# Loading E alone on the hardware queues, F through the casting queue, one early layer matmul and a split last copy in a low-rank attention and hardswish kernel

## The chip, the cores and the metric

The kernel runs on one core of a Trainium2 chip. The metric is the device time of one execution in microseconds (us). The kernel before took 508.95 us (median of 3 runs, 508.8 to 509.43). Of each version one execution was also taken with the hardware profiler; its span, from the first to the last instruction, is about 2 us shorter than the time of that execution (506.4 us of 508.28 for the kernel before).

Engines are named as in the profile: PE is TensorE, PEld its weight loads, ACT ScalarE, DVE VectorE, POOL GpSimd and SP SyncE. "The software queue" is the DMA queue that GpSimd fills (q0); q1 and q10 are the hardware queues that SyncE and ScalarE issue to.

## The reference, cut to what matters

```python
# q, k, v: (8, 8, 1024, 64);  E, F: (64, 1024);  w_in: (512, 2048);  w_out: (2048, 512), all float32
k_proj = einsum('ks,bhsd->bhkd', E, k)
v_proj = einsum('ks,bhsd->bhkd', F, v)
attn   = softmax(q @ k_proj.T / 8)
x      = (attn @ v_proj), heads side by side: (8192, 512)
h      = x @ w_in
out    = (h * clip(h + 3, 0, 6) / 6) @ w_out
```

Nearly all the work is the two matmuls of the layer. Attention of a batch is computed while the layer of the batch before it runs. Only the first batch has nothing to hide behind: before its first layer matmul stand the loads of E, F, k, q, v and w_in, and a chain of small matmuls.

## The kernel before

E and F are loaded uncast into the two halves of one tile, one on each hardware queue. The copies cast both at once, and eight transposes turn both at once. Before that, 12 filler matmuls on a tile of ones keep TensorE working while the loads come.

```python
scratch = g_tile().rearrange("p f n -> p (f n)")
ef_f32 = scratch[:, :2 * S].bitcast(f32)
nc.sync.dma_start(out=ef_f32[:KP], in_=E)
nc.scalar.dma_start(out=ef_f32[KP:], in_=F)
# ... cut
def busy(n):
    ps = pmm()
    for _ in range(n):
        nc.tensor.matmul(ps, ones[:, :P], ones, start=True, stop=True)

busy(12)
# ... cut; the software queue casts float32 to bfloat16 as it loads:
for j in range(KO):
    load_pair("k", j)
    load_q0(0, slice(2 * j, 2 * j + 2))
    if j == 0:
        make_identity(nc, ident)
for j in range(KO):
    load_pair("v", j)
# ... cut: then w_in in seven slices, the rest of q, w_out in four, k, v, q of the next batch
nc.vector.tensor_copy(ef_raw[:, :S // 2], ef_f32[:, :S // 2])
nc.scalar.copy(ef_raw[:, S // 2:], ef_f32[:, S // 2:])
# ... cut: eight transposes into ef_ps, then
nc.vector.tensor_copy(e_t, ef_pv[:, 0])
for a in range(2):
    nc.scalar.copy(f_t[:, :, a, :], ef_pv[:, 1])
busy(2)
```

The first block takes the four pairs of heads in turn, with fillers where TensorE would stand:

```python
for j in range(KO):
    self.keys(j)
    if j > 1:
        sums(j - 2)
    self.queries(0, (j,))
    if j > 0:
        scores(j - 1)
    else:
        busy(1)
    self.keys_transposed(j)
    if j < 2:
        busy(1)
scores(KO - 1)
# ... cut: values, sums and products of the pairs
products(2)
self.vals(3, nc.scalar.copy)
busy(1)
products(3)
```

The last tile of rows is computed in two halves of 256 columns. VectorE copies the first out of PSUM, ScalarE the second, and each has a store of its own:

```python
for e, copy, dma in ((0, nc.vector.tensor_copy, nc.sync), (1, nc.scalar.copy, nc.scalar)):
    half = slice(e * d_model // 2, (e + 1) * d_model // 2)
    o_ps = pmm()[:, :d_model // 2]
    for fo in range(FO):
        nc.tensor.matmul(o_ps, g[:, fo, c * P:(c + 1) * P], w_out_sb[:, fo, half],
                         start=(fo == 0), stop=(fo == FO - 1))
    o_sb = opool.tile([P, d_model], f32, tag="o_sb", name="o_sb")[:, :d_model // 2]
    copy(o_sb, o_ps)
    dma.dma_start(out=o_dst[:, half], in_=o_sb)
```

The softmax here doesn't subtract the row's maximum and nothing guards it: scores larger than these inputs give would overflow.

Of the kernel before, what the change touches and what calls it, by code (L numbers as in the profile page):

```python
# [8 lines left out]
f32 = mybir.dt.float32  # L9
# [6 lines left out]
def kernel(  # L16
# [49 lines left out]
    def pmm():  # L66
        return ps_mm.tile([P, TOK], f32, tag="mm", name="mm")

    def pat():
        return ps_at.tile([P, TOK], f32, tag="at", name="at")  # L70
# [3 lines left out]
        return gpool.tile([P, FO, TOK], bf16, tag="g", name="g")  # L74

    scratch = g_tile().rearrange("p f n -> p (f n)")
    ef_f32 = scratch[:, :2 * S].bitcast(f32)
    nc.sync.dma_start(out=ef_f32[:KP], in_=E)
    nc.scalar.dma_start(out=ef_f32[KP:], in_=F)
    nc.scalar.preload_act_table_set("natural_log_exp_and_others")  # L80
    ones = consts.tile([P, TOK], bf16, name="ones")
    nc.vector.memset(ones, 1.0)
# [7 lines left out]
    def busy(n):  # L90
        ps = pmm()
        for _ in range(n):
            nc.tensor.matmul(ps, ones[:, :P], ones, start=True, stop=True)  # L93

    busy(12)

    def raw_tile(name):
        return kqv_pool.tile([P, H, SO, D], bf16, tag=name, name=name)
# [13 lines left out]
    for j in range(KO):  # L112
        load_pair("k", j)
        load_q0(0, slice(2 * j, 2 * j + 2))
        if j == 0:
            make_identity(nc, ident)
    for j in range(KO):
        load_pair("v", j)

# [9 lines left out]
        nc.gpsimd.dma_start(out=w_in_sb[:, :, lo:lo + n], in_=w_in_v[:, :, lo:lo + n])  # L129

    for lo, n in ((0, 128), (128, 128), (256, 256), (512, 256), (768, 256),
                  (1024, 512), (1536, 512)):
        load_w_in(lo, n)
    load_q0(1, slice(0, H))
    for i in range(SB):
# [4 lines left out]

    e_t = consts.tile([P, SO, KP], bf16, name="e_t")
    f_t = consts.tile([P, SO, 2, KP], bf16, name="f_t")
    ef_raw = scratch[:, 2 * S:3 * S]
    nc.vector.tensor_copy(ef_raw[:, :S // 2], ef_f32[:, :S // 2])
    nc.scalar.copy(ef_raw[:, S // 2:], ef_f32[:, S // 2:])
    ef_si = ef_raw.rearrange("r (si so) -> r so si", so=SO)
    ef_ps = pat().bitcast(bf16)
    for so in range(SO):
        nc.tensor.transpose(ef_ps[:, so * P:(so + 1) * P], ef_si[:, so, :], ident)
    ef_pv = ef_ps.rearrange("p (so e r) -> p e so r", so=SO, e=2)  # L150
    nc.vector.tensor_copy(e_t, ef_pv[:, 0])
    for a in range(2):
        nc.scalar.copy(f_t[:, :, a, :], ef_pv[:, 1])
    ef_t = [e_t, f_t[:, :, 0, :]]
    busy(2)

# [198 lines left out]
    class First:  # L355
# [67 lines left out]
            return self.quads(lambda r, h: self.vp[r:r + KP, h, :], t, j, alloc)  # L423


        def first_block(self):
            recs = {}

            def scores(j):
# [15 lines left out]
# [7 lines that stand above are left out]
                else:  # L452
                    busy(1)
                self.keys_transposed(j)
                if j < 2:
                    busy(1)
            scores(KO - 1)
            self.vals(0, nc.vector.tensor_copy)
# [6 lines left out]
            busy(1)  # L465
            products(2)
            self.vals(3, nc.scalar.copy)
            busy(1)
            products(3)


# [40 lines left out]
    def second_group(b, t, g, c, copy=None):  # L512
        o_dst = out_rows(b, t, c)
        if (b, t, c) == (B - 1, NB - 1, SB - 1):

            for e, copy, dma in ((0, nc.vector.tensor_copy, nc.sync), (1, nc.scalar.copy, nc.scalar)):
                half = slice(e * d_model // 2, (e + 1) * d_model // 2)
                o_ps = pmm()[:, :d_model // 2]
                for fo in range(FO):
                    nc.tensor.matmul(o_ps, g[:, fo, c * P:(c + 1) * P], w_out_sb[:, fo, half],  # L520
                                     start=(fo == 0), stop=(fo == FO - 1))
                o_sb = opool.tile([P, d_model], f32, tag="o_sb", name="o_sb")[:, :d_model // 2]
                copy(o_sb, o_ps)
                dma.dma_start(out=o_dst[:, half], in_=o_sb)
            return
        o_ps = pmm()
        for fo in range(FO):
            nc.tensor.matmul(o_ps, g[:, fo, c * P:(c + 1) * P], w_out_sb[:, fo, :],  # L528
                             start=(fo == 0), stop=(fo == FO - 1))
            if fo % SB == SB - 1:  # L530
                yield
        o_sb = opool.tile([P, d_model], f32, tag="o_sb", name="o_sb")
        (copy or nc.scalar.copy)(o_sb, o_ps)  # L533
        nc.sync.dma_start(out=o_dst, in_=o_sb)
# [8 lines left out]

    xT = x_tile()
    first = First(xT)
    first.first_block()
    x_next = x_tile()
    g = [g_tile(), g_tile()]


    def two_groups(xT, t, g, kos):
        tiles = [pmm(), pmm()]
        for part in kos:
            for fo in range(2):
                h_part(tiles[fo], xT, t, fo, part)
        for fo in range(2):
            h_out(tiles[fo], g, fo)

    two_groups(xT, 0, g[0], ((0, 1, 2), (3,)))
    for fo in range(2, FO):  # L560
        first_group(xT, 0, g[0], fo)
        if fo >= FO - 2:
# [10 lines left out]
    for i in range(SB + 1):  # L573
# [3 lines left out]
            first.second_scores()  # L577
        elif i < 3:
            first.second_values(2 * i - 2)
    two_groups(xT, 1, g[1], ((0, 1), (2, 3)))  # L580
    for fo in range(2, FO):
        first_group(xT, 1, g[1], fo)
        pop()
# [19 lines left out]
    for b in range(1, B):  # L603
# [33 lines left out]
        for t in range(NB):  # L637
# [3 lines left out]
            for fo in range(FO):  # L641
                if b < 3 and t == 0 and fo < 2:

                    if fo == 0:
                        two_groups(xT, t, g, ((0, 1, 2), (3,)))
                else:
                    first_group(xT, t, g, fo)
                pop()
# [47 lines left out]
```

## Time and profile before

| | before |
|---|---|
| time, median | 508.95 us |
| span of the profiled run | 506.4 us |
| PE busy | 499.8 us (99%) |
| first keys start | 8.08 us |
| layer matmuls start and go on without a stop | 20.70 us |
| last matmul ends to the end of the span | about 3.3 us |

A line of the timeline gives start and length in us, the engine, the source line, the operation, output and input tiles, the number of instructions, and in brackets how long the engine stood idle before and what released it.

All that TensorE waited for in the whole span, from the view of waits (waiter, what released it, us in total, times, longest):

```profile
PE mm L93 <- DVE halves L84: 1.5, 1, 1.5
PE mm L414 <- ACT aT L434: 0.6, 1, 0.6
PE mm L407 <- DVE kT L377: 0.3, 1, 0.3
PE mm L528 <- DVE g L501: 0.2, 1, 0.2
```

### The profile page before, as it was taken

Reading aid. Unit: us, or ns where it says so; the run is one execution under the profiler, and the core shown is the slowest. Engines: PE = TensorE matmul, PEld = TensorE weight load, DVE = VectorE, ACT = ScalarE, POOL = GpSimd, SP = SyncE. Lnnn points to the kernel's source line nnn. Section 1 sums busy time; section 2 is a strip of 40 time slices with the busy share of each in tenths; the row PEclk is TensorE's granted clock in tenths of the full one; section 3 lists DMA queues with packets and bytes.
Section 4 is the critical chain, followed back from the end, with each engine's and each line's share of the span. In section 5 each row is a group of like instructions: output and inputs, shape, how many; then the busy total and the mean of one; then the engine's idle time right before and its main releaser. Section 6 shows DMA issues by size and latency. Waiting matters only on the chain.

```text
span 506.4 us, 7084 instructions
## 1 busy us (share of the span) xinstructions
PE 499.8 (99%) x2779; PEld 225.3 (44%) x2779; DVE 246.2 (49%) x384; ACT 256.2 (51%) x438; POOL 37.9 (7%) x57
## 2 busy tenths in 40 slices
PE   8999999999999999999999999999999999999997
PEld 4444444444444444444444444444444444444444
DVE  3572836865733564536635455534652446334420
ACT  3656466567565444654555544654455544434431
POOL 8610020020020020010002000000000000000000
PEclk9999999999999999999999999999999999999999
DMA  9999999599299998699316990248110361101112
GB/s 168 200 205 207 204 153 238 104 151 190 86 154 187 271 150 168 137 160 256 107 43 130 215 263 30 60 99 208 41 43 29 84 159 43 41 22 42 43 42 83
DMA packets 77529, 66.02 MB, mean 130 GB/s; under 512 B 36200, under 2 KB 66664, under 8 KB 77496
## 3 DMA queue, kind: packets, MB, share of 16 engines
q0 software_dynamic: 31952, 29.36, 37.1%
q1 hardware_dynamic: 45320, 35.82, 27.1%
q10 hardware_dynamic: 224, 0.39, 0.3%
q8 instruction: 21, 0.34, 0.3%
q14 instruction: 12, 0.10, 0.1%
HBM read 69.73 MB, written 16.94 MB: 171 GB/s over the span
## 4 chain that ended last, share of the span: by engine, by line
PE 96%; ACT 2%; DVE 1%; issue 0%; ACTq 0%
PE mm L528 43%; PE mm L495 43%; PE at L195 2%; PE mm L93 1%; PE at L244 1%; PE at L226 1%; PE mm L244 1%; PE mm L520 1%; PE mm L264 1%; ACT aT L235 0%; PE at L382 0%; PE at L414 0%; PE mm L226 0%; PE at L394 0%; PE mm L195 0%; PE at L366 0%
## 5 line engine op out<-in xcount | busy, mean ns | idle before, releaser
L501 DVE SCALAR_TENSOR_TENSOR g<-r,mm 128x512 bf16<-128x512 f32 x256 | 174.5, 687 | 176.3 <-ACT r L500 175.6
L495 PE MATMUL mm<-xT,w_in_sb 128*128 128x512 bf16 x1024 | 231.0, 379 | 0.3
L528 PE MATMUL mm<-w_out_sb,g 128*128 128x512 bf16 x1008 | 230.4, 379 | 0.2 <-DVE g L501 0.2
L500 ACT ACTIVATE r<-mm 128x512 f32<-128x512 f32 x256 | 152.3, 599 | 76.9 <-PE mm L495 75.7
L495 PEld LDWEIGHTS <-w_in_sb 128*128 128x128 bf16 x1024 | 99.3, 98 | 122.6 <-issue 4.0
L528 PEld LDWEIGHTS <-g 128*128 128x128 bf16 x1008 | 96.8, 98 | 120.3 <-issue 7.0
L533 ACT COPY o_sb<-mm 128x512 f32<-128x512 f32 x55 | 32.1, 586 | 124.0 <-PE mm L528 124.0
L257 DVE TENSOR_TENSOR xT<-at,rec 128x512 bf16<-128x512 f32 x42 | 26.5, 682 | 6.5 <-ACT rec L176 6.5
L235 ACT ACTIVATE aT<-at 128x512 bf16<-128x512 f32 x38 | 20.2, 615 | 9.1 <-PE at L226 9.1
L201 DVE CAST kp<-at 64x512 bf16<-64x512 f32 x12 | 7.7, 677 | 15.5 <-PE at L195 15.5
L216 POOL COPY mark<-qT 1x1 bf16<-1x1 bf16 x4 | 0.7, 177 | 161.6 <-DMA qT<-q 161.6
L235 ACT ACTIVATE aT<-mm 128x512 bf16<-128x512 f32 x18 | 10.3, 613 | 3.6 <-PE mm L226 3.6
L533 DVE COPY o_sb<-mm 128x512 f32<-128x512 f32 x8 | 5.5, 687 | 13.4 <-PE mm L528 13.4
L195 PE MATMUL at<-v,f_t 128*64 128x512 bf16 x48 | 11.5, 382 | 0.0
L195 PE MATMUL at<-k,e_t 128*64 128x512 bf16 x48 | 11.5, 382 | 0.0
L257 DVE TENSOR_TENSOR xT<-mm,rec 128x512 bf16<-128x512 f32 x14 | 9.0, 685 | 4.3 <-PE mm L244 4.3
L176 ACT ACTIVATE rec<-rec 128x1024 f32<-128x1024 f32 x10 | 10.6, 1061 | 0.3
L170 ACT ACTIVATE rec<-mm 128x512 f32<-128x512 f32 x10 | 5.5, 595 | 7.9 <-PE mm L244 5.4
L93 PE MATMUL mm<-ones 128*128 128x512 bf16 x19 | 7.8, 539 | 1.5 <-DVE halves L84 1.5
L170 ACT ACTIVATE few<-mm 128x512 f32<-128x512 f32 x10 | 5.4, 594 | 7.4 <-PE mm L264 7.4
L195 PEld LDWEIGHTS <-e_t 128*64 128x64 bf16 x56 | 5.6, 109 | 6.6 <-issue 1.9
L204 DVE CAST vp<-at 64x512 bf16<-64x512 f32 x12 | 8.3, 694 | 0.4
(75 smaller groups left out, 161.9 us busy)
## 6 DMA issues: line engine op xcount, KB each, us to landing
out_dram<-o_sb SPq DMA_DIRECT2D x63, 256.0 KB, 2.7
rec<-rows SPq DMA_DIRECT2D x40, 256.0 KB, 6.3
k<-in_k_dram POOLq DMA_DIRECT2D x7, 1024.0 KB, 14.2
v<-in_v_dram POOLq DMA_DIRECT2D x7, 1024.0 KB, 21.1
q<-in_q_dram POOLq DMA_DIRECT2D x7, 1024.0 KB, 10.3
w_out_sb<-in_moe_w_out_dram POOLq DMA_DIRECT2D x4, 512.0 KB, 17.3
k<-in_k_dram POOLq DMA_DIRECT2D x4, 256.0 KB, 5.4
v<-in_v_dram POOLq DMA_DIRECT2D x4, 256.0 KB, 7.7
```

Of the source, the lines that this page charges most:

```text
L93: nc.tensor.matmul(ps, ones[:, :P], ones, start=True, stop=True)
L170: nc.scalar.activation(rec[:, i], den, AF.Ln)
L176: nc.scalar.activation(flat, flat, AF.Exp, scale=-1.0)
L195: nc.tensor.matmul(ps[e * KP:(e + 1) * KP], ef_t[e][:, so, :], kqv[self.b]["kv"[e]][:, :, so, :], start=(so == 0), stop=(so == SO - 1))
L235: nc.scalar.activation(self.aT[j][:, r].rearrange("p a n -> p (a n)"), tiles[r], AF.Exp, scale=scale)
L244: nc.tensor.matmul(tiles[t][c:c + D].rearrange("p (r n) -> p r n", r=2), stationary(r, 2 * j + a), self.aT[j][r:r + KP, :, a, :], start=Tr ...
L257: nc.vector.tensor_mul(self.xT[:, j, t, :], av[t], rec[:, t])
L495: nc.tensor.matmul(h_ps, w_in_sb[:, ko, fo * P:(fo + 1) * P], xT[:, ko, t, :], start=(ko == 0), stop=(ko == KO - 1))
L500: nc.scalar.activation(r, h_ps, AF.Relu, bias=0.5, scale=1.0 / 6.0)
L501: nc.vector.scalar_tensor_tensor(g[:, fo, :], r, 1.0, h_ps, op0=ALU.min, op1=ALU.mult)
L528: nc.tensor.matmul(o_ps, g[:, fo, c * P:(c + 1) * P], w_out_sb[:, fo, :], start=(fo == 0), stop=(fo == FO - 1))
L533: (copy or nc.scalar.copy)(o_sb, o_ps)
```

## The change

The intent is to shorten the two ends. At the head, E alone uses both hardware queues, so that its transposes start sooner; F, which is needed only for values, goes through the casting software queue behind the first pair. Three of the 12 fillers go and two come in later. One layer matmul takes the place of the filler before the last values. At the tail, two engines share the last copy.

```diff
-    ef_f32 = scratch[:, :2 * S].bitcast(f32)
-    nc.sync.dma_start(out=ef_f32[:KP], in_=E)
-    nc.scalar.dma_start(out=ef_f32[KP:], in_=F)
+    for half, dma in zip(e_half, (nc.sync, nc.scalar)):
+        dma.dma_start(out=e_f32[:, half], in_=E[:, half])
...
-    busy(12)
+    busy(9)
...
             make_identity(nc, ident)
+            nc.gpsimd.dma_start(out=f_raw, in_=F)
...
-                  (1024, 512), (1536, 512)):
+                  (1024, 256), (1280, 256), (1536, 512)):
...     (E cast by both engines and transposed alone)
+    nc.vector.tensor_copy(e_t, with_sequence_on_partitions(e_raw))
+    busy(2)
+    def f_transposed():
+        ps = with_sequence_on_partitions(f_raw)
+        for a in range(2):
+            nc.scalar.copy(f_t[:, :, a, :], ps)
     busy(2)
...     (in the first block)
-                if j < 2:
+                if j == 0:
+                    f_transposed()
+                elif j < 2:
                     busy(1)
...
-            busy(1)
+            meanwhile()          # early[0].part(0, (0,)): one layer matmul
             products(3)
...     (the last tile)
-            for e, copy, dma in ((0, nc.vector.tensor_copy, nc.sync), (1, nc.scalar.copy, nc.scalar)):
+            ways = (nc.vector.tensor_copy, nc.sync), (nc.scalar.copy, nc.scalar)
+            for lo, pieces in ((0, ((0, half),)), (half, ((0, quarter), (quarter, half)))):
...
+                for (start, end), (copy, dma) in zip(pieces, ways):
+                    copy(o_sb, o_ps[:, start:end])
```

More of the change, by code (lines that the diff above doesn't have):

```diff
@@ L76 @@
     scratch = g_tile().rearrange("p f n -> p (f n)")
-    ef_f32 = scratch[:, :2 * S].bitcast(f32)
-    nc.sync.dma_start(out=ef_f32[:KP], in_=E)
-    nc.scalar.dma_start(out=ef_f32[KP:], in_=F)
+    e_f32 = scratch[:KP, :2 * S].bitcast(f32)
+    e_raw, f_raw = scratch[:KP, 2 * S:3 * S], scratch[:KP, 3 * S:4 * S]
+    e_half = [slice(i * S // 2, (i + 1) * S // 2) for i in range(2)]
+    for half, dma in zip(e_half, (nc.sync, nc.scalar)):
+        dma.dma_start(out=e_f32[:, half], in_=E[:, half])
     nc.scalar.preload_act_table_set("natural_log_exp_and_others")
@@ L142, with with_sequence_on_partitions @@
     f_t = consts.tile([P, SO, 2, KP], bf16, name="f_t")
-    ef_raw = scratch[:, 2 * S:3 * S]
-    nc.vector.tensor_copy(ef_raw[:, :S // 2], ef_f32[:, :S // 2])
-    nc.scalar.copy(ef_raw[:, S // 2:], ef_f32[:, S // 2:])
-    ef_si = ef_raw.rearrange("r (si so) -> r so si", so=SO)
-    ef_ps = pat().bitcast(bf16)
-    for so in range(SO):
-        nc.tensor.transpose(ef_ps[:, so * P:(so + 1) * P], ef_si[:, so, :], ident)
-    ef_pv = ef_ps.rearrange("p (so e r) -> p e so r", so=SO, e=2)
-    nc.vector.tensor_copy(e_t, ef_pv[:, 0])
-    for a in range(2):
-        nc.scalar.copy(f_t[:, :, a, :], ef_pv[:, 1])
+    for half, copy in zip(e_half, (nc.vector.tensor_copy, nc.scalar.copy)):
+        copy(e_raw[:, half], e_f32[:, half])
+    def with_sequence_on_partitions(raw):
+        ps = pat().bitcast(bf16)[:, :SO * KP]
+        for so in range(SO):
+            nc.tensor.transpose(ps[:, so * KP:(so + 1) * KP], raw.rearrange("r (si so) -> r so si", so=SO)[:, so, :],
+                                ident[:KP, :KP])
+        return ps.rearrange("p (so r) -> p so r", so=SO)
+    nc.vector.tensor_copy(e_t, with_sequence_on_partitions(e_raw))
[4 more added lines that the diff above has]
+            nc.scalar.copy(f_t[:, :, a, :], ps)
     ef_t = [e_t, f_t[:, :, 0, :]]
@@ L423, in values, with first_block @@
             return self.quads(lambda r, h: self.vp[r:r + KP, h, :], t, j, alloc)
-        def first_block(self):
+        def first_block(self, meanwhile):
             recs = {}
@@ L514, in second_group @@
         if (b, t, c) == (B - 1, NB - 1, SB - 1):
-            for e, copy, dma in ((0, nc.vector.tensor_copy, nc.sync), (1, nc.scalar.copy, nc.scalar)):
-                half = slice(e * d_model // 2, (e + 1) * d_model // 2)
-                o_ps = pmm()[:, :d_model // 2]
+            half, quarter = d_model // 2, d_model // 4
+            ways = (nc.vector.tensor_copy, nc.sync), (nc.scalar.copy, nc.scalar)
+            for lo, pieces in ((0, ((0, half),)), (half, ((0, quarter), (quarter, half)))):
+                o_ps = pmm()[:, :half]
                 for fo in range(FO):
-                    nc.tensor.matmul(o_ps, g[:, fo, c * P:(c + 1) * P], w_out_sb[:, fo, half],
+                    nc.tensor.matmul(o_ps, g[:, fo, c * P:(c + 1) * P], w_out_sb[:, fo, lo:lo + half],
                                      start=(fo == 0), stop=(fo == FO - 1))
-                o_sb = opool.tile([P, d_model], f32, tag="o_sb", name="o_sb")[:, :d_model // 2]
-                copy(o_sb, o_ps)
-                dma.dma_start(out=o_dst[:, half], in_=o_sb)
+                for (start, end), (copy, dma) in zip(pieces, ways):
+                    o_sb = opool.tile([P, d_model], f32, tag="o_sb", name="o_sb")[:, :end - start]
+                    copy(o_sb, o_ps[:, start:end])
+                    dma.dma_start(out=o_dst[:, lo + start:lo + end], in_=o_sb)
             return
@@ L545, with __init__, part, parts @@
     first = First(xT)
-    first.first_block()
-    x_next = x_tile()
-    g = [g_tile(), g_tile()]
-    def two_groups(xT, t, g, kos):
-        tiles = [pmm(), pmm()]
-        for part in kos:
-            for fo in range(2):
-                h_part(tiles[fo], xT, t, fo, part)
-        for fo in range(2):
-            h_out(tiles[fo], g, fo)
-    two_groups(xT, 0, g[0], ((0, 1, 2), (3,)))
+    g = [g_tile(), g_tile()]
+    class TwoGroups:
+        def __init__(self, xT, t, g):
+            self.xT, self.t, self.g = xT, t, g
+            self.tiles = [pmm(), pmm()]
+        def part(self, fo, kos):
+            h_part(self.tiles[fo], self.xT, self.t, fo, kos)
+        def parts(self, *kos):
+            for some in kos:
+                for fo in range(2):
+                    self.part(fo, some)
+            self.out()
+        def out(self):
+            for fo in range(2):
+                h_out(self.tiles[fo], self.g, fo)
+    early = []
+    def meanwhile():
+        early.append(TwoGroups(xT, 0, g[0]))
+        early[0].part(0, (0,))
+    first.first_block(meanwhile)
+    x_next = x_tile()
+    early[0].part(0, (1, 2))
+    early[0].part(1, (0, 1, 2))
+    for fo in range(2):
+        early[0].part(fo, (3,))
+    early[0].out()
     for fo in range(2, FO):
@@ L579 @@
             first.second_values(2 * i - 2)
-    two_groups(xT, 1, g[1], ((0, 1), (2, 3)))
+    TwoGroups(xT, 1, g[1]).parts((0, 1), (2, 3))
     for fo in range(2, FO):
@@ L644 @@
                     if fo == 0:
-                        two_groups(xT, t, g, ((0, 1, 2), (3,)))
+                        TwoGroups(xT, t, g).parts((0, 1, 2), (3,))
                 else:
```

## The prediction

> **What bounds the kernel now.** I read the page's busy shares first, then the chain that ended last, then TensorE's waits, and only then the two ends of the span.
>
> ```profile
> PE 499.8 (99%) x2779; PEld 225.3 (44%) x2779; DVE 246.2 (49%) x384; ACT 256.2 (51%) x438; POOL 37.9 (7%) x57
> PE 96%; ACT 2%; DVE 1%; issue 0%; ACTq 0%
> ```
>
> TensorE (PE) is busy 99% of 506.4 us, and 96% of the chain runs through it. TensorE's waits over the whole span add up to 2.6 us, of which 1.5 us is the wait before its first instruction. So nothing in the middle, from about 21 to 500 us, can give much, and the diff changes nothing there. Only the head and the tail are left. The head in the chain, in order of time (start us, us, what):
>
> ```profile
> 1.46 5.30 PE mm L93 x12
> 6.76 0.81 PE at L149 x8
> ...
> 7.60 0.44 DVE e_t L151
> ...
> 8.08 0.63 PE at L366 x8
> ...
> 19.45 0.57 PE at L382 x8
> ...
> 20.05 0.28 ACT vp L385
> ...
> 20.36 0.40 PE at L414 x2
> 20.77 7.45 PE mm L495 x34
> ```
>
> L93 are filler matmuls that only keep TensorE working; they are "busy" without being work, which is why 99% hides a head. The real chain is: E and F land, are cast, are transposed (L149), copied (e_t), keys (L366) and so on, until the layer's matmuls (L495) start and never stop. What the change is worth is how much sooner L495 runs without a stop. What feeds the head is seen in the loads (time to landing last) and in the queues of the stretches 2.0 to 3.4, 3.4 to 4.4 and 4.4 to 5.0 us (packets, MB, share):
>
> ```profile
> g<-in_F_dram ACTq DMA_DIRECT2D x1, 256.0 KB, 5.0
> w_in_sb<-in_moe_w_in_dram POOLq DMA_DIRECT2D x1, 128.0 KB, 9.5
> ...
> q1 hardware_dynamic: 57, 0.23, 90.2%
> ...
> q10 hardware_dynamic: 58, 0.24, 97.9%
> ...
> q0 software_dynamic: 83, 0.08, 84.5%
> ```
>
> E (q1) moves first, then F (q10), and only behind them the software queue with k, q, v and the weights. F was issued at 0.74 us, so it landed at 5.74. The software queue then runs full until past 30 us, at some 205 GB/s of what it writes. The first slice of w_in was issued at 10.67 us and landed near 20.2; it is used at 20.70. So **the head has a second bound close beside TensorE: the software queue**. Issue plus landing time against first use gives small slack everywhere: third key pair 10.4 against 11.46, fourth 12.4 against 13.08, third value pair 17.0 against 17.84, fourth 18.15 against 19.39, first w_in slice 20.2 against 20.70, the slice for groups 8 to 11 27.0 against about 27.6.
>
> **What the Trainium skill says.** "TensorE: Matmul & The Clock Gate", Part 1, says that TensorE starts at half its clock and is released after a free-running window of some 3.4 us in which it was busy. The trace agrees: fillers start every 0.43 us up to 6.13 us, and two after 7.39 us are 0.22 us apart; the release came near 7.37 us. Part 4 of that page says that transposes do not count as busy in the same way; this trace does not test it. "DMA: Bandwidth & Descriptors", section "Issuing engines are not separate DMA queues", says that DMAs from different engines run on the same 16 DMA engines. The trace agrees: E and F, issued together, moved one after the other. The same page, "SWDGE vs HWDGE vs iDMA", says that only GpSimd's DMA can cast, which is why F's cast load goes behind the first key pair there.
>
> **The change part by part.**
>
> 1. E alone, in halves on both hardware queues. E's packets were done near 3.75 us and F's near 4.86; F's landing was seen at 5.74, 0.9 us later. With E alone the last packet is near 3.7 us, so I estimate landing at 4.6. The casts (VectorE 0.66 us, ScalarE 0.62; same length along the row, half the partitions) end at 5.26. Nine fillers end at 1.46 + 9 x 0.427 = 5.30, which fits. The eight transposes start near 5.30 in place of 6.57: **1.27 us earlier**.
>
> 2. Part of that is given back at once. The clock is still at half there. Eight transposes at 0.107 us bring TensorE to 6.16; then stand four fillers in place of two: three at half clock, the last partly at full, until about 7.62. Keys follow there instead of at 8.08: **0.46 us earlier**. (e_t, ready at about 6.8, is not the limit then.) Had the clock been released earlier, fillers would be 0.22 us each and it would be up to 1.0; later, about 0.3.
>
> 3. F's own eight transposes replace one filler after the first keys: about 8 x 0.056 = 0.45 us (key matmuls' spacing at full clock) against 0.22 us and 0.1 us of idling there: 0.13 us lost. The two f_t copies (1.07 us on ScalarE) move from 8.06 to about 9.7 and end near when the first exponential needs ScalarE (11.01 before). **Net so far 0.33 us.** From there to the values the order is the same, so it is carried on.
>
> 4. The software queue. It starts after E instead of after F: some 0.8 to 1.1 us sooner. It then carries F itself, 256 KB read, 0.62 us at the rate of E's packets (4 x 0.155 us per DMA engine). Starting sooner it may also run thin at first, so I take a net shift of 0.3 us earlier for all behind F. w_in's first slice then lands near 19.9. GpSimd's issue for F (0.74 us) delays later issues, but they were 2 us or more ahead of their turn.
>
> 5. One layer matmul (0.216 us) replaces the filler before the last values, under the wait for the copy of vp (0.28 us). It is real work done where a filler ran: **0.22 us gained**, if w_in's first slice has landed. The copy would be done near 20.0; the slice lands at 19.9, so the matmul ends near 20.12 and costs about 0.1 us. Rest of L495 then near 20.46 with one already done: 0.24 + 0.22 = **about 0.45 us of head**.
>
> 6. Splitting the 512-column slice of w_in lets groups 8 and 9 start on 256 columns: removes a wait that would arise (slack 0.6 us before) and is worth nothing by itself.
>
> 7. The tail:
>
> ```profile
> 501.43 0.42 DVE L523 COPY o_sb<-mm 128x256 f32<-128x256 f32 x1 [14.30 <-PE mm L520]
> ...
> 503.16 0.37 ACT L523 COPY o_sb<-mm 128x256 f32<-128x256 f32 x1 [2.91 <-PE mm L520]
> 503.56 0.35 ACTq L524 DMA_DIRECT2D out_dram<-o_sb  x1
> ```
>
> The last copy (0.37 us for 256 columns on ScalarE) becomes 128 columns on each of two engines. From 512 columns 0.586 and 256 columns 0.37, 128 columns is about 0.26 on ScalarE; on VectorE (0.687, 0.42) about 0.29. Gain **0.08 us**; the bytes to store are the same, in packets of half the size, so the store (1.8 us to landing) gains nothing sure. I take 0.1.
>
> Sum: 0.45 + 0.1 = 0.55, and with some chance that the queue or clock is kinder, 0.65 us. 508.95 - 0.65 = **508.3 us**.
>
> **The rivals.**
>
> A. *Full gain.* The 1.27 us of the head reach the end, with 0.22 and 0.1 added: 1.6 us, 507.35. For it: three fillers gone and no other long wait. Against it: two more fillers, F's transposes back in the chain, and w_in's first slice, which no part of the change brings 1.3 us sooner. I give this or near it 8%.
>
> B. *The software queue takes the place of the wait removed.* F now stands in it ahead of three key pairs. If the queue does not start sooner, because GpSimd's descriptors are not ready, everything behind F lands 0.6 us later: w_in's first slice near 20.8. The early layer matmul would then hold up the last values behind it, and the head would be 0.3 to 0.4 us longer: 509.2. For it: slack of 0.5 to 1 us only. Against it: other starts of this queue in the trace show packets 1.6 us after the issue, so at 1.24 + 1.6 = 2.8 us it was ready and had to wait behind F. 12%.
>
> C. *The clock.* Fewer matmuls lie in the window that released the clock (9 fillers, transposes, then 4). If that window no longer counts as busy, the release comes 3.4 us later, near 10.8, and the work between costs about 1.2 us more: 509.6. The two added fillers speak against it. 10%.
>
> D. *All hidden.* Were the software queue the only bound, only parts 4, 5 and 7 count: 0.3 + 0.1, 508.5. That is inside my range.
>
> **Range and chances.** 2% is 10.2 us, and the whole head and tail that the change touches are some 20 us and 3 us, almost all of it work that stays. No rival comes near 2%: within 2% has 0.99. The three runs before spread over 0.6 us, which the moving clock window may cause. The range 507.6 to 508.95 holds the middle case, D and part of A, and leaves B and C outside on the slow side.
>
> **What would show it.** Transposes of E should start near 5.3 us and the first keys near 7.6; F should land before 8.5 us; the first w_in slice near 19.9, with TensorE at most 0.3 us idle before the early layer matmul; L495 unbroken from about 20.5. In the middle each matmul group takes as long as before. The last copies should take 0.26 and 0.29 us. The prediction is wrong if E lands after 5 us, if the fillers at full clock start only after 10 us, or if slices of w_in hold up L495.

## More of the kernel before

The timeline of the kernel before, TensorE alone, at four places that the change is to move: first keys, third keys, first layer matmuls, and the first projection of the second batch's values.

```profile
8.08 0.63 PE L366 MATMUL at<-k,e_t 128*64 128x128 bf16 x8
...
11.46 0.63 PE L366 MATMUL at<-k,e_t 128*64 128x128 bf16 x8
...
20.70 1.04 PE L495 MATMUL mm<-xT,w_in_sb 128*128 128x512 bf16 x4
...
55.29 0.40 PE L195 MATMUL at<-v,f_t 128*64 128x512 bf16 x1
```

None of the four has a bracket: TensorE went from one to the next without waiting there.

## The result

The changed kernel took **509.67 us** (median of 6 runs, 508.91 to 511.92), against 508.88 us for the kernel before in 6 runs (507.95 to 509.43). The ratio is **1.0026**, with a 95% interval of 1.0002 to 1.0049. Ratios here are the mean time of one kernel's fast runs over that of the other's of the same rounds, so they are not quite the ratio of the medians. By the 2% rule this is "same", as expected. But the time is above the range: the change costs about 0.8 us by the medians where 0.65 us was to be gained.

The six runs are of two kinds. Four had a mean granted clock of 1.0 and took 508.91 to 509.84 us; two had 0.99 and took 511.12 and 511.92 us. All count as fast runs of one core. Averaged, the four are 0.57 us above the mean of before (509.34 against 508.77); the two slow ones bring the mean to 1.30 us above it. So there are two losses to explain. (The first turns out to have two parts, one in the loads and one in the tail, after the end of the span.)

The profile after is of a run at full clock (509.1 us, span 507.0). TensorE at the same four places, with one more wait (9.94) and with the keys beside the second batch's values (55.28), in its timeline:

```profile
7.25 0.63 PE L376 MATMUL at<-k,e_t 128*64 128x128 bf16 x8
...
9.94 0.40 PE L404 MATMUL at<-ident,q 128*128 128x128 bf16 x4 [0.19 <-DMA q<-in_q_dram]
...
11.45 0.61 PE L376 MATMUL at<-k,e_t 128*64 128x128 bf16 x8 [0.72 <-DMA k<-in_k_dram]
...
20.83 3.41 PE L507 MATMUL mm<-xT,w_in_sb 128*128 128x512 bf16 x15
...
55.28 0.40 PE L205 MATMUL at<-k,e_t 128*64 128x512 bf16 x1
55.94 0.38 PE L205 MATMUL at<-v,f_t 128*64 128x512 bf16 x1 [0.26 <-DMA v<-in_v_dram]
```

The first keys start 0.83 us sooner. By the third keys that is gone: 11.45 against 11.46 us, after a wait of 0.72 us for a load. The layer runs on from 20.83 us with one matmul done before it (20.70 before, with none). That is not yet a loss: at the first transposes in the middle of the layer (33.58 us, 33.66 before) this execution is 0.08 us ahead. It loses at 55.94 us, where the profile before has no wait. The bracket there, 0.26, counts only from the modelled end of the matmul before; the first matmul of the values starts 0.66 us after that of the keys, where before both start at 55.29. The layer goes on at 57.76 us (57.14 before), and that is the whole 0.6 us by which this span is the longer one. Other executions lose at other loads: in the profiles of e1, e4 and e8 nothing waits near 55 us, but the same transposes start at 34.81, 34.80 and 34.21 us.

TensorE's waits for loads in the changed kernel, from the view of waits:

```profile
PE at L376 <- DMA k<-in_k_dram: 0.7, 1, 0.7
...
PE at L205 <- DMA v<-in_v_dram: 0.3, 1, 0.3
...
PE at L404 <- DMA q<-in_q_dram: 0.2, 1, 0.2
```

The third pair of keys, as issued and with its time to landing, in the kernel before and then after (timeline of GpSimd, and the loads):

```profile
4.72 0.73 POOL L110 DMA_DIRECT2D k<-in_k_dram  x1
...
k<-in_k_dram POOLq DMA_DIRECT2D x1, 256.0 KB, 5.7
```

```profile
5.29 0.72 POOL L112 DMA_DIRECT2D k<-in_k_dram  x1
...
k<-in_k_dram POOLq DMA_DIRECT2D x1, 256.0 KB, 6.0
```

It landed at 4.72 + 5.7 = 10.4 us before, and at 5.29 + 6.0 = 11.3 us after: 0.9 us *later*, although the queue's first packet moved at 3.05 us in place of 4.45.

In the trace the semaphore of each load goes up 16 times; I read this as once for each of the 16 DMA engines when its share has landed. TensorE goes on only after the last (third keys: 11.32 us, start at 11.45). These increments (us; first engine / eighth / last):

| load | before | after |
|---|---|---|
| first keys | 6.13 / 6.22 / 6.46 | 4.80 / 4.88 / 5.55 |
| second keys | 8.10 / 8.29 / 8.38 | 7.48 / 7.71 / 8.73 |
| third keys | 10.04 / 10.21 / 10.38 | 9.99 / 10.41 / 11.32 |
| fourth values | 17.83 / 18.00 / 18.19 | 17.92 / 18.29 / 19.41 |
| first w_in slice | 18.56 / 18.73 / 20.14 | 18.66 / 19.02 / 20.13 |
| second batch's values | 51.37 / 51.58 / 53.76 | 51.76 / 52.52 / 55.90 |

The head start of 1.3 us at the first keys is lost by the third even for the first engine. F's load, estimated at 0.62 us in the prediction, would explain half of that. The other half, and the spread between the engines, comes with single packets that take long. Of the software queue's packets before 20 us, 17 took over 0.4 us after the change (up to 1.37 us, most of them around 6 and 8 us), and none before it.

The tail, in the changed kernel's timeline:

```profile
503.79 0.29 DVE L537 COPY o_sb<-mm 128x128 f32<-128x128 f32 x1 [1.32 <-PE mm L533]
...
504.16 0.27 ACT L537 COPY o_sb<-mm 128x128 f32<-128x128 f32 x1 [3.29 <-DVE o_sb L537]
504.46 0.35 ACTq L538 DMA_DIRECT2D out_dram<-o_sb  x1
```

The two copies do not run side by side: ScalarE's waits for VectorE's, since both read one PSUM tile (with a tile each, in e3 below, it waits for TensorE alone). The last store is issued 0.76 us after the last matmul (503.70), not 0.48 us as before. It is half as large, and the span ends sooner after its issue (2.54 us in place of 2.81), so within the span the whole tail is about 3.3 us long in both. What follows the span is another matter (e1 and e2).

### The profile page after: what moved, and what is told of

It is laid out like the page before. It is cut to its first block, busy times and chain, and to the rows that moved or that the text cites. A ratio compares the mean times of both kernels' runs of the same rounds, so it can differ in the third digit from the quotient of the medians.

```text
span 507.0 us, 7049 instructions
## 1 busy us (share of the span) xinstructions
PE 495.7 (98%) x2733; PEld 225.5 (44%) x2784; DVE 246.3 (49%) x385; ACT 256.1 (51%) x438; POOL 39.2 (8%) x59
## 4 chain that ended last, share of the span: by engine, by line
PE 86%; DMA 9%; POOL 2%; issue 1%; ACT 1%; DVE 1%; DVEq 0%; ACTq 0%; POOLq 0%
PE mm L542 41%; PE mm L507 38%; DMA v<-in_v_dram 7%; PE at L205 2%; DMA w_in_sb<-in_moe_w_in_dram 2%; PE at L254 1%; PE at L236 1%; PE mm L254 1%; PE mm L533 1%; POOL q L108 1%; PE mm L274 1%; POOL k L112 1%; ACT aT L245 0%; PE mm L236 0%; PE mm L205 0%
## 5 line engine op out<-in xcount | busy, mean ns | idle before, releaser
L542 PE MATMUL mm<-w_out_sb,g 128*128 128x512 bf16 x985 | 227.6, 379 | 1.9 <-issue 1.0
```

## The experiments

Medians are of 5 or 6 runs, each beside runs of the kernel before on the same chip in the same rounds.

| run | median, us | before there, us | ratio to before (95%) |
|---|---|---|---|
| changed kernel, first measurement | 509.67 | 508.88 | 1.0026 (1.0002 to 1.0049) |
| e8, changed kernel again | 509.05 | 508.53 | 1.0010 (0.9998 to 1.0023) |
| e1, changed, old tail | 508.85 | 508.02 | 1.0006 (0.9992 to 1.0020) |
| e2, before, new tail | 508.88 | 508.02 | 1.0007 (0.9992 to 1.0022) |
| e4, changed, 12 fillers | 509.18 | 508.02 | 1.0011 (0.9997 to 1.0024) |
| e5, changed, F behind the keys | 510.31 | 508.02 | 1.0039 (1.0024 to 1.0055) |
| e7, changed, F on a hardware queue | 508.68 | 508.53 | 0.9994 (0.9979 to 1.0010) |
| e9, before, early layer matmul | 508.62 | 508.53 | 0.9998 (0.9985 to 1.0011) |
| e11, changed, more fillers | 508.91 | 508.53 | 1.0005 (0.9992 to 1.0017) |
| e3, before, tail in two tiles | 508.63 | 508.13 | 1.0003 (0.9989 to 1.0017) |
| e10, e9 and that tail | 508.36 | 508.13 | 0.9999 (0.9986 to 1.0013) |
| e12, changed, F loaded twice | 509.18 | 508.13 | 1.0030 (1.0009 to 1.0051) |
| e13, e7 and that tail | 508.14 | 508.13 | 0.9999 (0.9983 to 1.0016) |
| e14, before, half loads (wrong result) | 508.11 | 508.47 | 0.9995 (0.9976 to 1.0014) |
| e15, changed, half loads (wrong result) | 507.13 | 508.47 | 0.9971 (0.9955 to 0.9987) |

### The tail: e1 and e2

In e1 the changed kernel gets back the tail of before; in e2 the kernel before gets the new tail.

```diff
 e1: the changed kernel
-            for lo, pieces in ((0, ((0, half),)), (half, ((0, quarter), (quarter, half)))):
+            for e, copy, dma in ((0, nc.vector.tensor_copy, nc.sync), (1, nc.scalar.copy, nc.scalar)):
 e2: the kernel before, the other way round
```

> The changed kernel with the tail of before. In the changed kernel's profile the two last copies ran one after the other (0.29 us, then 0.27 us), but the smaller last stores landed sooner, so the tail as a whole came out about even. Theory (the tail is not the loss): within 0.15 us of the changed kernel, so 0.3 to 1 us slower than before. Rival (the tail is the loss): as fast as before or 0.3 us faster than it. In both, the first keys still start near 7.3 us and the third keys wait for their load.

> The kernel before with the new tail alone. Theory (tail about even): within 0.2 us of before. Rival (the serial copies cost): 0.3 us or more slower than before. The profile should show ScalarE's last copy starting only when VectorE's last copy has ended.

Both came out at 1.0006 and 1.0007, neither clear of 1 nor of each other. e2's profile shows ScalarE's last copy starting after VectorE's as in the changed kernel, and its span ends about 3.3 us after its last matmul too. So within the span the tail is about even, and its predicted 0.1 us did not come.

But the time has a part outside the span. The record lists time and span of every run of the experiments and of the changed kernel, and their difference goes with the tail. With the two last stores of before it is 1.80 us in the median of 88 runs (76 of them under 2.0; 1.72 to 3.43). With three last stores, as in the changed kernel, e2, e8, e11 and the other new tail of e3, e10 and e13, it is 2.12 us in the median of 37 runs, and 2.04 to 2.56 in all of them. On each of the three chips that ran both, the medians are 0.3 to 0.4 us apart. So the new tail costs about 0.3 us after the end of the span, and it is part of the loss. e2 shows it alone: its mean span is that of before (506.60 against 506.61), its mean time is 0.42 us longer. What the 0.3 us is spent on, no profile shows.

e1, with the old tail, is 0.36 us longer than before in its mean span and 0.33 us in its mean time. This is the head's part. Its interval holds 1, so these times alone do not settle that the head loses.

### F behind the keys: e5

```diff
             make_identity(nc, ident)
-            nc.gpsimd.dma_start(out=f_raw, in_=F)
+    nc.gpsimd.dma_start(out=f_raw, in_=F)
     for j in range(KO):
         load_pair("v", j)
...
-                if j == 0:
-                    f_transposed()
-                elif j < 2:
+                if j < 2:
                     busy(1)
+            f_transposed()
             scores(KO - 1)
```

> The changed kernel (old tail), with F's casting load moved behind all pairs of keys and queries and its transposes to just before the values. Theory of the queue: in the changed kernel F's issue pushed the issue of the second to fourth pairs back by 0.56 us while the queue had started 1.4 us sooner, so the queue ran dry near 6 and 8 us (packets of up to 1.37 us, the second key pair done 1.9 us after F) and never got that back. Here the third key pair should land near 9.6 us in place of 11.3, the third keys do not wait, the value load of the second batch lands before 54 us, and the time is 0.5 to 1 us below the changed kernel. Rival (the queue is bound by its bytes, F anywhere costs 0.62 us): the first w_in slice lands as late as in the changed kernel (20.1 us), and the time does not change.

It was the slowest, 1.0039, and my theory missed. The first DMA engine did have the third keys early (9.20 us against 10.04 before), but the last had them at 10.86 us, with 13 packets over 0.4 us. So F's place and its issue ahead of the other keys are not what alone makes packets slow. The profile shows a second harm: the values waited 1.4 us for F's copies, and then the clock was lost. The view of busy time by stretch (stretch, its length, busy us and count of PE, PEld, DVE, ACT, POOL, then the clock, DMA share and GB/s):

```profile
13.70:17.10 3.40, 1.93 (x26) 1.25 (x26) 0.93 (x4) 2.88 (x8) 2.39 (x4) 1.00 1.24 204
17.20:20.50 3.30, 3.30 (x27) 2.03 (x25) 0.87 (x3) 1.89 (x5) 1.57 (x3) 0.50 1.53 190
20.60:24.00 3.40, 3.26 (x26) 1.45 (x24) 2.63 (x5) 1.06 (x3) 2.94 (x4) 1.00 1.46 196
```

In the stretch from 13.7 us TensorE worked 1.93 of 3.4 us; in the next its clock is 0.50. All six runs of e5 had a mean clock of 0.997 or 0.993. One stretch of 3.41 us at half clock takes 0.0034 off the mean over 507 us, so 0.997 is one lost stretch and 0.993 is two.

### The clock: e4, e8 and e11

e4 brings back the 12 fillers, e8 is the changed kernel again, and e11 adds fillers where TensorE waited.

```diff
 e4, with the old tail
-    busy(9)
+    busy(12)
 e11
             for j in range(KO):
+                if j > 0:
+                    busy(2 if j == 2 else 1)
                 self.keys(j)
```

> The changed kernel (old tail) with 12 fillers as before in place of 9, which undoes the earlier start of the transposes and nothing else. Theory of the clock: the runs of 511 us and more of the changed kernel had a mean clock of 0.99, so in them the release of the clock came a window of 3.4 us later; with 12 fillers no run is at 0.99, the spread is that of before (1.5 us or less) and the median is at or below that of the run with 9 fillers. Rival (the clock plays no part): the spread and the runs at 0.99 stay, and the median is the same as with 9 fillers since the software queue sets the time.

> The changed kernel itself, unaltered, to see whether its slow runs come back. Theory (clock lost again in the head): TensorE waits longer for loads there, and where a stretch of 3.4 us holds more than about 1 us of waiting the clock is halved for the next stretch; so some of the six runs show a mean clock of 0.998 or less, and those are the slower ones, by 1 to 3 us. Rival (chance of that chip): all runs between 508 and 509.5 and clocks at 0.999 or 1.0, as with the old tail.

> The changed kernel with fillers where it waited for loads: one before the second and fourth keys, two before the third. Theory of the clock: no run shows a mean clock under 0.998, and the median is 0.3 us or more below that of the changed kernel on the same chip, though each filler costs up to 0.22 us. Rival (the loads alone set the time): clocks and median stay within 0.2 us of the changed kernel, or it is slower by the fillers.

e4 did not confirm what I expected of it: two of its runs show 0.996 and 0.997, although it had all its fillers. Its release came at 5.24 us and the clock was lost at 12.07, after a wait of 0.9 us for the third keys. So the missing fillers at the start are not what loses the clock; the waits for loads further on are at least a candidate.

e8 took 1.0010, with one run of five at 0.996, its profiled one. There TensorE waited 1.0 us for the third keys, and the clock was halved from 11.54 to 14.95 us. But that run took 509.02 us, no more than the others: a lost stretch where loads are waited for anyway costs little. Slow runs near 511 us did not come back in these rounds.

e11 had no run under 0.999, as expected of it, and took 508.91 us against 509.05 for e8 in the same rounds. That is less than the 0.3 us expected, and inside the noise. They do not give the loss back. That they hold the clock is not shown either, with no run of five against one of five in e8.

A slow run was caught in the profile of e12 (below), at 511.54 us. Its busy time by stretch:

```profile
4.70:11.40 6.70, 5.80 (x56) 3.42 (x54) 2.58 (x9) 1.69 (x5) 6.54 (x10) 1.00 1.25 187
11.50:21.60 10.10, 9.30 (x71) 5.54 (x72) 3.15 (x11) 5.78 (x13) 6.56 (x9) 0.50 1.37 199
21.80:25.00 3.20, 3.06 (x24) 1.34 (x22) 2.42 (x5) 0.95 (x3) 2.20 (x4) 1.00 1.45 196
```

Here half clock lasted for three stretches, 11.45 to 21.69 us. TensorE had waited 0.6 us for keys before, and waited 0.7 us more from 11.27 us, across the edge. The two runs of e12 at 0.99 took 511.51 and 511.54 us, the four others 508.88 to 509.37: the lost clock costs some 2.5 us there. The changed kernel's two slow runs have the same clock and a similar extra time (1.8 and 2.6 us above the mean of the four). That they are of this kind is inferred from that, since neither was profiled.

Taken over all profiles, five of the nine with the changed head and all its loads show a lost stretch (e4, e5, e7, e8, e12), and none of the five with the head of before. Not every loss follows a wait for a load: before that of e5 (at 17.13 us) TensorE had waited 1.4 us for F's copies, and in the 3.4 us before that of e7 (at 15.45 us) 0.4 us for ScalarE's exponentials and 0.3 us for a copy. In no run of the kernel before beside these experiments was the mean clock under 0.999.

### F away from the software queue, and F twice: e7 and e12

In e7 F is loaded uncast behind E on SyncE's queue and cast by ScalarE. e12 keeps F in the software queue and loads it a second time, unused, on the hardware queue.

```diff
 e7, with the old tail
-            nc.gpsimd.dma_start(out=f_raw, in_=F)
+    f_f32 = scratch[:KP, 4 * S:6 * S].bitcast(f32)
+    nc.sync.dma_start(out=f_f32, in_=F)
+    nc.scalar.copy(f_raw, f_f32)
 e12, with the old tail
+    nc.sync.dma_start(out=f_f32, in_=F)        # and the load by GpSimd stays
```

> The changed kernel (old tail) with F loaded uncast on a hardware queue behind E and cast by ScalarE, so that F is not in the software queue and the software queue starts behind F as before. Theory (what the queue loses it loses because it starts closer behind its issues): no packet of the first pairs takes over 0.5 us, the key pairs land as in the kernel before (third pair at 10.4, fourth at 12.4, within 0.3 us), and although the first keys start near 7.3 us TensorE then waits for the pairs; time within 0.4 us of before. Rival (F's place in the software queue is the loss): pairs land 0.6 us or more before those of the kernel before, and the time is 0.5 us or more below it.

> The changed kernel (old tail) with F kept in the software queue, and F loaded a second time, unused, on a hardware queue behind E, only to delay the start of the software queue as before. Theory A (the slow packets come from starting the queue close behind its issues): at most 3 packets over 0.4 us before 20 us (10 to 25 in the versions that started near 3.0), and the fourth key pair lands 0.6 us after that of the version with F on a hardware queue alone, near 13.2, which is where the changed kernel had it although its queue started earlier. Theory B (F inside the software queue causes them): 10 or more slow packets stay.

e7 came out as its theory had it, but for the start: the software queue's first packet moved at 2.96 us, beside F, not behind it. The rest holds nearly: 0.9994, two packets over 0.4 us (one of 0.62, where none over 0.5 was expected), third keys at 10.74 and fourth at 12.64 us (10.38 and 12.43 before). The loads come about when they came before, and by its times so does the end, although E is transposed over a microsecond sooner. In its profile something else is mixed in: the first values start at 15.40 us, 0.6 us ahead of before, but then TensorE runs at half clock from 15.45 to 18.86, and the third and fourth values land later (18.33 and 19.00 us, 16.95 and 18.19 before).

e12 was meant to delay the software queue's start and failed in that: its first packet moved at 3.0 us all the same, with 28 slow packets. So it does not tell theory A from B. Together with e13 (below), which has F outside the software queue, a first packet at 3.07 us and 11 slow ones, it rules out F's place as the only cause. In the heads with full loads, those that started the queue at 4.1 us or later had 0 to 5 slow packets; those that started near 3 us had 2 (e7) and otherwise 10 or more. What a slow packet waits for, no run shows.

### Early layer matmul alone: e9

```diff
 the kernel before
-            busy(1)
+            meanwhile()          # one layer matmul
             products(3)
```

> The kernel before with one part of the change alone: one layer matmul in place of the filler ahead of the last values. The first w_in slice lands at 20.1 us there and the filler's place is free until 20.33 us, so it should gain its 0.22 us: 0.1 to 0.3 us faster than before. Rival (the next w_in slices set the pace, landing at 20.5 and 21.75 with 0.35 us of slack and less): no gain, within 0.1 us.

0.9998: the rival was right that nothing is gained that the times can show. In its profile the fourth values waited 0.6 us for their load, which landed at 19.69 us (18.19 in the profile of before). This is not the early matmul's doing: in e2, e3 and e10, which also have the head of before, this load landed at 19.69, 19.78 and 19.72 us and TensorE waited 0.6 us too. So the one profile of before that the prediction was made from, with this load at 18.19, is the exception among five. That load was late on one DMA engine: the eighth had it at 18.09. An instruction fetch of 16 KB took 0.97 us at 17.58 us, the only other traffic on the DMA engines then. Every profile with full loads has such a fetch at 16 to 18 us, and most a load that ends late on one engine soon after. That the fetch delays that engine is my reading of the times, not shown.

### A better tail, and a version meant to beat both: e3, e10 and e13

The last two quarters get PSUM tiles of their own: the first is copied while the second is multiplied.

```diff
+            for lo, n, copy, dma in ((0, half, nc.vector.tensor_copy, nc.sync),
+                                     (half, quarter, nc.vector.tensor_copy, nc.sync),
+                                     (half + quarter, quarter, nc.scalar.copy, nc.scalar)):
+                o_ps = pmm()[:, :n]
```

> The kernel before with a tail whose last two quarters have PSUM tiles of their own, so that the first quarter is copied while the second is still multiplied and no copy waits for the other. From the profiles: the copy of 128 columns takes 0.27 us in place of 0.37, and the smaller last store landed 0.27 us sooner after its issue. Theory: 0.2 to 0.4 us faster than before; the profile ends 2.9 to 3.1 us after the last matmul in place of 3.3. Rival (more stores, more overhead at the end): within 0.1 us.

> That tail and the early layer matmul on the loads of before. The early matmul alone gave nothing. Theory: as the tail alone, 0.2 to 0.4 us faster than before. Rival: the early matmul costs, since a late w_in slice holds up the last values: 0.1 us or more slower than the tail alone.

> The version meant to beat both: F on a hardware queue behind E and the tail with a tile for each quarter. Theory: 0.2 to 0.6 us faster than before (0.9988 to 0.9996) and 0.7 us or more faster than the changed kernel; the interval may still hold 1. Rival: no better than before, because lost clock in the head eats it; mean clocks under 0.998 would show that.

The profile of e3 has what was wanted:

```profile
503.65 0.27 ACT L524 COPY o_sb<-mm 128x128 f32<-128x128 f32 x1 [2.95 <-PE mm L521]
503.94 0.35 ACTq L525 DMA_DIRECT2D out_dram<-o_sb  x1
```

The copy waits for TensorE alone, and the span ends at 506.5 us, 2.9 us after the last matmul at 503.57, where it was 3.3. But the times do not show this 0.35 us: 1.0003 for e3, 0.9999 for e10 and e13. The early matmul neither gains nor costs with it. All three intervals are 0.0026 or more wide, so 0.35 us (0.0007) can't be told from nothing. Besides, these tails have three last stores, and their runs pay the 0.3 us outside the span (above), which is about what the tail gains inside it. Against the changed kernel, e13 is ahead by its ratio (0.9999 against 1.0010 and 1.0026, in other rounds); against the kernel before, no version tried has a proven gain.

### Half the loads: e14 and e15

All this shows where the gain went in profiles. To test it as a cause, e14 and e15 load half of the first batch's keys and values and use that half twice. The results are wrong; TensorE's instructions stay the same, and the loads run ahead.

```diff
-        nc.gpsimd.dma_start(out=kqv[0][n][:, hs], in_=kqv_dram[n][0][:, hs])
+        nc.gpsimd.dma_start(out=kqv[0][n][:, hs, :SO // 2], in_=kqv_dram[n][0][:, hs, :SO // 2])
...
-    kqv[0]["k"][:, 2 * j:2 * j + 2, so, :]
+    kqv[0]["k"][:, 2 * j:2 * j + 2, so % (SO // 2), :]      # and so for "v"
```

> The kernel before with half of the first batch's keys and values loaded; the result is wrong on purpose. Both theories: the kernel before hardly waited for loads in the head, so the time stays within 0.4 us of before; the first w_in slice lands some 2.5 us sooner, near 17.6.

> The changed kernel (old tail) with the same half loads; the result is wrong on purpose. Theory (waits for loads, and the clock lost through them, eat the gain): 0.5 to 1.0 us faster than the kernel before with half loads, no wait of TensorE for keys or values over 0.2 us, no run with a mean clock under 0.998, and the layer matmuls start without a stop 0.5 us or more sooner. Rival (TensorE's own chain gives the gain back): within 0.2 us of it.

With loads out of the way the change works. The kernel before took 508.11 us, the changed kernel with the old tail 507.13 us. The ratio of the two, from the means of their six runs each in the same rounds, is 0.9977, a gain of 1.2 us; the slowest run of the one (507.5) is below the fastest of the other (507.83). The clock was released in both profiles near 6.6 us, so they compare well. First e14, then e15: start of the layer, and of the first transposes in the middle of it (two answers of the timeline each).

```profile
20.40 0.82 PE L495 MATMUL mm<-xT,w_in_sb 128*128 128x512 bf16 x3
...
33.36 0.61 PE L394 MATMUL at<-ident,q 128*128 128x128 bf16 x8
```

```profile
20.09 1.25 PE L507 MATMUL mm<-xT,w_in_sb 128*128 128x512 bf16 x5
...
32.84 0.61 PE L404 MATMUL at<-ident,q 128*128 128x128 bf16 x8
```

The layer runs on 0.31 us sooner and has one matmul more behind it; at 33 us the lead is 0.52 us. Neither profile has a wait of TensorE for keys, queries or values. By the spans the gain is 0.83 us in the mean (505.38 against 506.22, all six of e15 below all six of e14). The rest of the 1.2 us lies outside the spans: two runs of e14 (508.59 and 509.32 us) took 2.5 and 2.9 us there, all others 1.7 to 2.0.

## Why the prediction was wrong

**The bound and where to look: right.** Head and tail alone changed. In the profiles before and after, the middle takes the same time apart from the one wait at 55.9 us, which is for a later load of the same queue.

**Parts 1 to 3, TensorE's own chain: right.** E's transposes started at 5.41 us (expected 5.30) and the first keys at 7.25 (7.62, with the clock released at 6.56 us in that run). F was transposed in 0.6 us. With half loads the head gained 0.52 us in the profile; parts 1 to 3 and 5 together give 0.33 + 0.22 = 0.55 where w_in's slice does not hold it up.

**Part 4, the software queue: the step that failed.** It says "I take a net shift of 0.3 us earlier for all behind F". The shift to the last DMA engine was 0.9 us *later* for the third keys and none for the first w_in slice (20.13 against 20.14). Two things were missed. First, the rate of the queue was read as if all 16 engines went in step, but a load lands with its slowest engine, and the spread grew from 0.34 to 1.33 us at the third keys. Second, I took the queue's early start to be a gain that lasts; instead the packets of the next pairs became slow. The slack table had the right threat (0.7 us at the fourth keys, 0.5 us at w_in) and part 4 stepped over it. It was also read from one execution: the fourth values had 1.2 us of slack there, and none in the four other profiles with that head.

**Part 5: about right in the profiles, not seen in times.** Its gain of 0.22 us hung on "if w_in's first slice has landed". In the profile after the slice landed at 20.13 us and the matmul's weights were loaded at 20.17; the layer went on 0.13 us later than before with one matmul (0.22 us) done, which makes the 0.08 us of lead. With half loads nothing held it up. Alone on the head of before it gave nothing by the times (e9, 0.9998).

**Part 6: right as far as it was tested.** No slice of w_in held up the layer noticeably in the profile after. It was not tested alone.

**Part 7, the tail: the second step that failed.** The copies were to run side by side; ScalarE's waited for VectorE's, which took 0.28 us more before the last issue, and the smaller store gave 0.27 us back. The predicted 0.1 us came out as about 0 within the span, and as 0.3 us lost after it, where the prediction did not look. The profile before shows such a wait, also of two copies out of one PSUM tile: ScalarE's copy of F's half starts when VectorE's of E's half has ended (7.60 + 0.42 us).

```profile
8.06 1.07 ACT L153 COPY f_t<-at 128x512 bf16<-128x512 bf16 x2 [1.67 <-DVE e_t L151]
```

**Rivals B and C** were given 12% and 10%. B is what happened in the head at full clock, in another form: loads take the place of the wait removed, though GpSimd's descriptors not being ready, its reason, is not shown. Of the 0.57 us by which the four runs are slower, about 0.3 us is the tail's, and only the rest is left for the loads. C had the right harm and the wrong place. The clock was released early enough in every profile (4.2 to 7.4 us) and lost again later, after waits. It adds about 0.7 us to the mean of the first measurement, through two runs of six; I read that part as chance, since in the later rounds (e8) it did not return, though e12 shows it again in two of six; this is not shown.

**Range.** 508.95 was too low an upper end. Runs of one kernel spread over 1 to 3 us, and a median of a few can sit anywhere in that.

What stays open: what a slow packet waits for, when waiting loses the clock and when not, and what the three-store tail spends its 0.3 us on after the span.

## What to carry to other kernels

Before a chain at the head of a kernel is shortened, compare the landing of every load with its first use, and take the landing from the slowest DMA engine; where slack is half a microsecond, a microsecond taken out of the compute came back as waits here. Read the slack from several executions, not from one. A cheap way to test it is to halve the loads on purpose and see if the gain appears. And waiting has a second price: after a stretch with about a microsecond of waiting, TensorE can run the next 3.4 us or more at half clock, so fillers that look like waste may be holding the clock (e11 was too few runs to show it). Last, compare the time of a run with its span: a tail that is even in the profile can still cost after it.

## What the Trainium skill lacked or had wrong

- "TensorE: Matmul & The Clock Gate", Part 1, has the clock fall back after an idle window of some 3.4 us, and its section "HAM oscillation — how this bites in real kernels" gives "no PE-idle gaps >~3.4µs" as the rule. Here it was lost in e8 with no wait over 1.0 us in the stretch before, with TensorE busy 2.19 of 3.42 us there, and in e12 at 2.69 of 3.42 us. No threshold is visible: the changed kernel kept its clock after a stretch with 2.56 us busy. That it stays lost in steps of 3.41 us (one step in e4, e5, e7 and e8, three in e12) fits the page's window. The page's section "A second HAM failure mode: psum-queue depth-cycling" does have a clock that comes and goes through short idles, but gives no threshold for it.
- "DMA: Bandwidth & Descriptors", section "Queues, rings and completion order", says that an engine takes turns between its queues packet by packet. In the kernel before, F's packets began at 3.44 us, when E's were nearly done (last at 3.53), and the software queue's at 4.45, when F's ended on the first engines, though the issues began at 0.74, 0.74 and 1.24 us. No packet-wise turns are seen there; in e7, where F followed E on one hardware queue, the software queue did move beside it from 2.96 us. The prediction took E before F as agreeing with the section "Issuing engines are not separate DMA queues"; it fits engines that are shared, but that section also has such DMAs interleave, which E and F did not.
- No page gives a time for how far the engines of one load fall out of step: here the last was up to 1.8 us behind the eighth for the full loads of the head (19.72 against 17.93 in e10), and 3.4 us for one of 1 MB (55.90 against 52.52).
- No page says that the time outside a kernel's span depends on its last stores: here it was 1.80 us in the median with two and 2.12 us with three (88 and 37 runs).
